# A gated recurrence with a multiplicative feed-forward: single PSUM banks for the first up product, two short leading chunks, a new division of copies among engines and a new written order

## The chip, the cores and the metric

The kernel runs on one core of one Trainium2 chip. A core has TensorE (PE: matrix products, its weight loads shown as PEld), VectorE (DVE), ScalarE (ACT), GpSimd (POOL), and SyncE (SP), which here issues almost all DMA transfers. The metric is the device time of one execution in microseconds; the median of five executions stands for the kernel.

## The reference

There are 4 sequences of 5,824 tokens with 256 channels, 23,296 tokens in all, in float32. First comes a recurrence over time, channel by channel, whose coefficients are gates:

```python
a_base = 1.0 / (1.0 + np.exp(-a_param))
log_a = c * sig_r * np.log(np.clip(a_base, 1e-06, 1.0 - 1e-06))[None, None, :]   # c = 8, sig_r = sigmoid(r_gate)
a_t = np.exp(log_a)
norm = np.sqrt(np.maximum(1.0 - a_t * a_t, 1e-06))
x_gated = norm * sig_i * x                                                       # sig_i = sigmoid(i_gate)
h = a_t[:, t] * h + x_gated[:, t]                                                # for every t, from h = 0
```

Its output, all h, goes through a feed-forward with a product in place of an activation; the widths are 256, 1024, 1024, 256:

```python
a = x @ w1
b = x @ w2
h = a * b @ w3
return (h @ w_out).astype(np.float32)
```

## The kernel before

**Tiles.** The tokens are cut into chunks: one of 256 and 45 of 512 (list `sizes`, L50). For the recurrence channels must lie on partitions and time along the row, so a chunk is held as two channel blocks of 128 partitions; `cb` counts them. The inputs come with tokens on partitions, so the two gate terms are turned by 128 x 128 blocks: on TensorE against an identity (`turn_pe`, L162) for the chunks in the sets `TURN_R` and `TURN_U`, and by a transposing DMA (`turn_dma`, L174) for the others.

**One chunk, step by step.** Each step has a letter in the order list. `r`, `i`, `x` load the inputs (L118). `R` and `I` are tanh of half the gates on ScalarE (a sigmoid is half of one plus such a tanh). `p` adds one (GpSimd), `t` multiplies by x in two halves (GpSimd; VectorE does both steps in one for the chunks in `DV_TIMES`). `V` and `U` turn the results. `d` is the decay, an exponential on ScalarE, whose per-channel rate stands in `la4`; `s` squares it (GpSimd, or VectorE where `DV_SQUARE` says so); `q` is the root of one minus the square (ScalarE); `g` multiplies by the turned gate (VectorE); `h` is the scan over time (VectorE, L214), which starts from the last column of the chunk before; `y` casts to bfloat16 (GpSimd, or VectorE for `DV_CAST`). The exponential and tanh on one side and the root on the other need different function tables of ScalarE, which are loaded at each turn from one to the other.

**Feed-forward of a chunk.** The 1,024 hidden columns are taken in four pairs of 128-column blocks; `mp` is the pair. `a` makes the pair of the first product with w1 (four matmuls of 128 x 128 weights and up to 512 tokens), `b` that with w2 (L240). `c` copies a finished `a` from PSUM to SBUF as bfloat16, on ScalarE or, for the pairs in `DV_COPY`, on VectorE (L256). `m` multiplies the copy by `b` straight from PSUM (VectorE, L262). `D` multiplies 128 tokens of the product by the folded matrix (8 matmuls of 256 columns, L269), `e` copies two such results out of PSUM (ScalarE, or VectorE for `DV_EVAC`), and `o` stores them. w3 and w_out aren't applied one after the other: at the start their product is computed once (`Ft`, `Fc`, `Fm`, `Fe`), and `D` uses that.

**PSUM.** [...] A ring of three double-bank tiles, `pab`, is shared by `a`, `b` and the warming matmuls (`warm`, L235); a ring of two single banks, `po`, serves the turns on TensorE, the folding and `D`. A tile is given out again after its reader is done, in the order of allocation.

**Order.** Nothing is scheduled automatically. `ORDER` is a written list of some 2,000 steps (2,450 in the changed kernel, where `a` and `c` come in halves); each engine takes its own instructions from it in exactly that order and waits at an instruction until its inputs, and its buffer, are ready. So the list settles what stands behind a late step on the same engine. Its beginning is `A0. r1 r0 i0 Lw3.0 x0 i1 A1. E R1 R0 x1 V0 V1 ...`, where `Lw`/`Cw` load and cast pieces of weights and `A0`, `A1`, `A2` compute the rates from `a_param`, which a small transfer on ScalarE's queue brings in single words, one per channel.

Of the kernel before, what the change touches and what calls it, by code (L numbers as in the profile page):

```python
# [10 lines left out]
F32 = mybir.dt.float32  # L11
# [11 lines left out]
def kernel(  # L23
# [26 lines left out]
    sizes = [256] + [CT] * 45  # L50
# [10 lines left out]
    psum = ctx.enter_context(tc.tile_pool(name="psum", bufs=3, space=bass.MemoryType.PSUM))  # L61
# [6 lines left out]
    la4 = consts.tile([P, NCB], F32, tag="la4")  # L68
    zz, zd, zt = (consts.tile([P, NCB], F32, name=tag, tag=tag) for tag in ("zz", "zd", "zt"))
# [9 lines left out]
    TURN_R = {0, 1, 2, 3, 4, 5, 7, 8, 13}  # L79
    TURN_U = {0, 1, 2, 3, 5, 8, 9}  # L80
    DV_TIMES = {0, 1, 2, 8}
    DV_PLUS = set()
    DV_HALF = set()
    DV_SQUARE = {(0, 0), (0, 1), (1, 0), (1, 1), (5, 0), (6, 0), (7, 1), (9, 1), (11, 0), (12, 0), (14, 0), (15, 1),
        (20, 1), (24, 1), (27, 0), (29, 0), (36, 0), (37, 0), (38, 0), (41, 0)}
    DV_CAST = {0, 20, 28, 37, 39, 40, 42, 45}
    DV_COPY = {(0, 3), (1, 1), (1, 3), (2, 1), (3, 2), (7, 2), (8, 0), (8, 1), (10, 0), (11, 1), (13, 0), (14, 0),
        (14, 2), (15, 3), (18, 1), (18, 3), (19, 3), (20, 3), (21, 3), (22, 3), (23, 1), (25, 0), (25, 2), (28, 1), (33,
        1), (33, 2), (36, 3), (40, 2), (41, 2), (41, 3), (44, 0), (45, 0)}
    DV_EVAC = {(0, 0), (1, 1), (2, 0), (2, 1), (3, 0), (4, 0), (4, 1), (5, 0), (6, 1), (7, 1), (8, 1), (9, 1), (10,  # L90
        0), (17, 0), (18, 1), (19, 0), (19, 1), (22, 0), (23, 1), (27, 0), (27, 1), (28, 1), (30, 0), (31, 0), (33, 1),
        (34, 1), (35, 0), (35, 1), (41, 1), (42, 0), (42, 1)}
    FOLD_ACT = {('c', 7), ('e', 0), ('e', 1), ('e', 4), ('e', 6), ('e', 7)}
    W_ACT = {('w2', 0), ('w3', 1), ('w3', 2), ('w3', 3)}
    W_DVE = {('w3', 0)}
    STAGE = {'w1': ['a', 'a'], 'w2': ['nrm', 'nrm'], 'wo': ['a', 'nrm'], 'w3': ['a', 'nrm', 'a', 'nrm', 'a', 'nrm',
        'a', 'nrm']}
    WARM = [30, 30, 24]
    src = {"r": rf, "i": jf, "x": xf}

    def flat(t):
        return t.rearrange("p cb j q -> p (cb j q)").rearrange("p (j d) -> p j d", d=D)

# [22 lines left out]
    def tanh_r(c):  # L126
# [4 lines left out]
        else:  # L131
            nc.scalar.activation(out=t.rearrange("p cb j q -> p j cb q"), in_=cut(T["r", c]),  # L132
# [9 lines left out]
    def plus(c):  # L142
        t = T["thi", c]
        (nc.vector if c in DV_PLUS else nc.gpsimd).tensor_scalar(t, t, 1.0, 1.0, op0=ALU.add, op1=ALU.mult)  # L144
# [384 lines left out]
```

## Time and profile before

| what | value |
|---|---|
| median of 5 executions | 522.42 us (520.72 to 524.76) |
| the profiled execution | 523.5 us, span of the core 521.7 us |
| TensorE busy | 502.2 us (96% of the span) |
| VectorE busy | 479.8 us (92%) |
| ScalarE busy | 429.6 us (82%) |
| GpSimd busy | 299.3 us (57%) |
| DMA traffic | 123.28 MB, mean 236 GB/s; 83.8% of the 16 DMA engines' time on SP's queue |

The span is what the profiler saw on the core, from the first instruction to the last; the execution's own time is a little longer. A group in the profile reads: line, engine, operation, output<-inputs, sizes and count, then busy time and mean duration of one in ns, then the engine's idle time before these and what ended it. In a list of waits each row says who waited for whom: us in total, times, longest. Busy time of TensorE includes the ends of matmuls that overlap with the next one.

### The profile page before, as it was taken

The numbers are of one execution on the slowest core, as the hardware profiler recorded it, in microseconds if no ns is written. First come the engines' busy times: TensorE is split into PE (matmuls) and PEld (weight loads), VectorE is DVE, ScalarE is ACT, GpSimd is POOL, SyncE is SP. The second block draws the span as 40 slices with busy tenths as digits, with TensorE's granted clock in tenths as the row PEclk, the third lists the DMA queues.
The fourth block names the chain that finished last, engine by engine and source line by source line (L and its number), as shares of the span: only waits on it lengthen the run. The fifth ranks groups of instructions, "written<-read, shape, count | busy, mean of one in ns | idle before, by whom it ended". The sixth has DMA issues, their size and how long they took to land.

```text
span 521.7 us, 8827 instructions
## 1 busy us (share of the span) xinstructions
PE 502.2 (96%) x3260; PEld 309.8 (59%) x3260; DVE 479.8 (92%) x456; ACT 429.6 (82%) x493; POOL 299.3 (57%) x251
## 2 busy tenths in 40 slices
PE   4899999999999999999999999999999999999997
PEld 4667655656565566566665556556556565656556
DVE  4899999999999999899999899999998999999973
ACT  6899997998898998999987997988977796766432
POOL 0668755786829674876566765757257756634000
PEclk9999999999999999999999999999999999999999
DMA  8999979899999886999979969999966978342113
GB/s 297 405 410 291 333 252 274 224 294 253 332 294 265 201 235 201 278 247 302 246 227 302 240 216 217 292 238 247 245 178 199 274 210 203 101 123 81 62 52 111
DMA packets 174604, 123.28 MB, mean 236 GB/s; under 512 B 84448, under 2 KB 170208, under 8 KB 174560
## 3 DMA queue, kind: packets, MB, share of 16 engines
q1 hardware_dynamic: 174288, 122.71, 83.8%
q8 instruction: 25, 0.41, 0.3%
q14 instruction: 19, 0.16, 0.1%
q10 hardware_dynamic: 272, 0.00, 0.0%
HBM read 78.91 MB, written 23.86 MB: 197 GB/s over the span
## 4 chain that ended last, share of the span: by engine, by line
PE 72%; DVE 15%; issue 6%; ACT 4%; DMA 2%; POOL 0%; SPq 0%; DVEq 0%; ACTq 0%; POOLq 0%
PE pb L246 23%; PE po L277 23%; PE pa L246 22%; DVE g_t L266 6%; DVE h_t L225 4%; DVE sa L252 1%; PE pw L342 1%; DVE nrm L210 1%; DMA i_t<-in_i_gate_dram 1%; ACT sa L254 1%; PE warm L238 1%; DMA la<-in_a_param_dram 1%; ACT a_t L188 1%; PE ptr L167 1%; DVE nrm L195 1%
## 5 line engine op out<-in xcount | busy, mean ns | idle before, releaser
L246 PEld LDWEIGHTS <-w_sb 128*128 128x128 bf16 x1472 | 143.0, 98 | 152.7 <-issue 12.7
L266 DVE TENSOR_TENSOR g_t<-sa,pb 128x1024 bf16<-128x1024 bf16 (+1 forms) x184 | 216.0, 1199 | 16.9 <-PE pb L246 10.7
L254 ACT CAST sa<-pa 128x1024 bf16<-128x1024 f32 (+1 forms) x152 | 149.7, 1004 | 55.0 <-PE pa L246 50.7
L246 PE MATMUL pb<-y_t,w_sb 128*128 128x512 bf16 (+1 forms) x736 | 180.2, 377 | 5.0 <-DVE g_t L266 2.5
L246 PE MATMUL pa<-y_t,w_sb 128*128 128x512 bf16 (+1 forms) x736 | 180.7, 377 | 3.5 <-DVE g_t L266 1.6
L277 PE MATMUL po<-wp_sb,g_t 128*128 128x256 bf16 x1456 | 179.4, 273 | 0.0
L277 PEld LDWEIGHTS <-g_t 128*128 128x128 bf16 x1456 | 142.4, 98 | 42.4 <-issue 0.2
L225 DVE TENSOR_TENSOR_SCAN h_t<-a_t,h_t,nrm 128x512 f32<-128x512 f32 (+3 forms) x90 | 117.7, 1334 | 1.2
L160 POOL TENSOR_TENSOR u_t<-th_i,x_t 128x512 bf16<-128x512 f32 x84 | 113.2, 1364 | 2.5 <-DMA ut<-u_t 1.3
L233 POOL CAST y_t<-h_t 128x1024 bf16<-128x1024 f32 x38 | 44.4, 1169 | 119.2 <-DVE h_t L225 102.6
L195 POOL TENSOR_TENSOR nrm<-a_t 128x512 f32<-128x512 f32 x72 | 85.5, 1200 | 20.7 <-ACT a_t L188 20.6
L144 POOL TENSOR_SCALAR th_i<-th_i 128x1024 f32<-128x1024 f32 x42 | 49.2, 1174 | 30.8 <-ACT th_i L139 30.7
L188 ACT ACTIVATE a_t<-rt,la 128x512 f32<-128x512 bf16 x74 | 59.1, 819 | 2.6 <-DMA rt<-th_r 1.5
L139 ACT ACTIVATE th_i<-i_t 128x1024 f32<-128x1024 f32 (+1 forms) x46 | 48.3, 1052 | 7.6 <-DMA i_t<-in_i_gate_dram 3.9
L210 DVE SCALAR_TENSOR_TENSOR nrm<-nrm,ut 128x1024 f32<-128x1024 f32 x39 | 52.7, 1354 | 0.0
L254 ACT COPY ot<-po 128x512 f32<-128x512 f32 (+1 forms) x60 | 34.7, 578 | 17.0 <-PE po L277 16.2
L199 ACT ACTIVATE nrm<-nrm 128x1024 f32<-128x1024 f32 (+1 forms) x46 | 46.9, 1048 | 0.3
L252 DVE CAST sa<-pa 128x1024 bf16<-128x1024 f32 (+1 forms) x32 | 38.3, 1198 | 5.6 <-PE pa L246 5.4
L132 ACT ACTIVATE th_r<-r_t 128x1024 bf16<-128x1024 f32 x37 | 39.3, 1061 | 0.1
L199 ACT ACT_TABLE_LOAD x20 | 25.7, 1283 | 1.7 <-DVE nrm L195 1.4
L252 DVE COPY ot<-po 128x512 f32<-128x512 f32 (+1 forms) x33 | 21.9, 665 | 4.0 <-PE po L277 4.0
L195 DVE TENSOR_TENSOR nrm<-a_t 128x512 f32<-128x512 f32 (+1 forms) x20 | 18.5, 931 | 0.9 <-ACT a_t L188 0.9
(51 smaller groups left out, 157.0 us busy)
## 6 DMA issues: line engine op xcount, KB each, us to landing
r_t<-in_r_gate_dram SPq DMA_DIRECT2D x45, 512.0 KB, 5.6
i_t<-in_i_gate_dram SPq DMA_DIRECT2D x45, 512.0 KB, 5.4
x_t<-in_x_dram SPq DMA_DIRECT2D x45, 512.0 KB, 5.5
out_dram<-ot SPq DMA_DIRECT2D x89, 256.0 KB, 3.6
wf<-in_moe_w_dram SPq DMA_DIRECT2D x12, 512.0 KB, 9.0
wf<-in_moe_w_out_dram SPq DMA_DIRECT2D x2, 512.0 KB, 11.5
ut<-u_t SPq DMA_TRANSPOSE x39, 4.9
rt<-th_r SPq DMA_TRANSPOSE x37, 4.5
```

The source lines that it names most:

```text
L144: (nc.vector if c in DV_PLUS else nc.gpsimd).tensor_scalar(t, t, 1.0, 1.0, op0=ALU.add, op1=ALU.mult)
L160: (nc.vector if (c, half) in DV_HALF else nc.gpsimd).tensor_mul(out=u, in0=t, in1=xt)
L188: nc.scalar.activation(out=a, in_=pr, func=AF.Exp, scale=la4[:, cb:cb + 1], bias=la4[:, cb:cb + 1])
L195: eng.tensor_mul(out=T["n", c][:, cb, :w], in0=T["a", c][:, cb, :w], in1=T["a", c][:, cb, :w])
L199: nc.scalar.activation(out=T["n", c][:, :, :w], in_=T["n", c][:, :, :w], func=AF.Sqrt, scale=-1.0, bias=1.0)
L210: nc.vector.scalar_tensor_tensor(out=T["n", c][:, :, :w], in0=T["n", c][:, :, :w], scalar=1e-3, in1=T["pu", c][:, :, :w], op0=ALU.max, op1 ...
L225: nc.vector.tensor_tensor_scan(T["h", c][:, cb, lo:hi], T["a", c][:, cb, lo:hi], T["n", c][:, cb, lo:hi], init, ALU.mult, ALU.add)
L246: nc.tensor.matmul(out=pp[:, q, :w], lhsT=w_sb[:, cb, m * P:(m + 1) * P], rhs=T["y", c][:, cb, :w], start=(cb == 0), stop=(cb == NCB - 1))
L252: nc.vector.tensor_copy(out=dst, in_=src_ps)
L254: nc.scalar.copy(out=dst, in_=src_ps)
L266: nc.vector.tensor_mul(out=T["g", c][:, 2 * mp:2 * mp + 2, :w], in0=T["sa", c, mp][:, :, :w], in1=T["pb", c, mp][:, :, :w])
L277: nc.tensor.matmul(out=po, lhsT=T["g", c][:, k, j * P:(j + 1) * P], rhs=wp_sb[:, k, :], start=(k == 0), stop=(k == KD - 1), skip_group_che ...
```

## The change

There are five parts.

1. **PSUM.** The ring of three double banks becomes two rings: `psum_a`, two single banks for halves of the first product, and `psum_b`, two double banks for the second product and the warming. The step `a` is issued in halves (`a12.0.1` is chunk 12, pair 0, half 1), and so is its copy `c`. The eight banks remain in use.
2. **Chunks.** The sizes are 256, 256, 44 times 512 and 256. So the first two chunks and the last are short, and there are 47. Several helpers take the chunk's length where they had the full one (`dense`, `plus`, `times`, `turn_dma`).
3. **Division of work.** ScalarE gets a list of squares, `AC_SQUARE` (17 of them). The sets for VectorE shrink: output copies from 33 to 5, squares from 20 to 4, casts of y from 8 to none, and first-product copies from 32 pairs to 44 halves, all in chunks 0 to 10. TensorE turns r for 7 chunks (9 before) and u for 6 (7 before). The casts of the weights move between engines.
4. **Rates.** `a_param` comes as two rows of 128 words, is turned on TensorE (`rates_turn`) and copied to `la4`. There are four sets of warming identity products (26, 16, 24, 36 matmuls; before 30, 30, 24).
5. **Order.** The whole list is new.

`CASTING` and `AC_CAST` are empty sets, so the branches that ask for them don't run.

```diff
-    sizes = [256] + [CT] * 45
+    sizes = [256, 256] + [CT] * 44 + [256]
...
-    psum = ctx.enter_context(tc.tile_pool(name="psum", bufs=3, space=bass.MemoryType.PSUM))
+    psum_a = ctx.enter_context(tc.tile_pool(name="psum_a", bufs=2, space=bass.MemoryType.PSUM))
+    psum_b = ctx.enter_context(tc.tile_pool(name="psum_b", bufs=2, space=bass.MemoryType.PSUM))
     psum_o = ctx.enter_context(tc.tile_pool(name="psum_o", bufs=2, space=bass.MemoryType.PSUM))
...
-    TURN_R = {0, 1, 2, 3, 4, 5, 7, 8, 13}
-    TURN_U = {0, 1, 2, 3, 5, 8, 9}
-    DV_TIMES = {0, 1, 2, 8}
+    TURN_R = {0, 1, 2, 3, 4, 7, 9}
+    TURN_U = {0, 1, 2, 3, 4, 7}
+    DV_TIMES = {0, 1}
...
+    DV_HALF = {(2, 0), (15, 0)}
+    DV_SQUARE = {(1, 0), (1, 1), (3, 1), (14, 1)}
+    AC_SQUARE = {(0, 0), (0, 1), (2, 0), (2, 1), (4, 0), (4, 1), (7, 0), (7, 1), (8, 0), (9, 1), (10, 1), (11, 1),
+        (12, 0), (13, 1), (14, 0), (15, 1), (16, 0)}
+    DV_CAST = set()
...
+    DV_EVAC = {(1, 0), (6, 0), (9, 0), (9, 1)}
...
-    W_ACT = {('w2', 0), ('w3', 1), ('w3', 2), ('w3', 3)}
-    W_DVE = {('w3', 0)}
+    W_ACT = {('w2', 1), ('w3', 4), ('w3', 7)}
+    W_DVE = {('w1', 0), ('w1', 1), ('w2', 0)}
...
-    WARM = [30, 30, 24]
+    WARM = [26, 16, 24, 36]
...
+        if (c, cb) in AC_SQUARE:
+            nc.scalar.activation(out=n, in_=a, func=AF.Square)
+        else:
+            (nc.vector if (c, cb) in DV_SQUARE else nc.gpsimd).tensor_mul(out=n, in0=a, in1=a)
...
+    def up(c, m, dst, w_sb):
+        w = sizes[c]
+        for cb in range(NCB):
+            nc.tensor.matmul(out=dst[:, :w], lhsT=w_sb[:, cb, m * P:(m + 1) * P],
+                             rhs=T["y", c][:, cb, :w], start=(cb == 0), stop=(cb == NCB - 1))
+
+    def up_a(c, mp, q):
+        T["pa", c, mp, q] = pp = psum_a.tile([P, CT], F32, name="pa", tag="pa")
+        up(c, 2 * mp + q, pp, w1_sb)
+
+    def up_b(c, mp):
+        T["pb", c, mp] = pp = psum_b.tile([P, 2, CT], F32, name="pb", tag="pb")
         for q in range(2):
...
+            up(c, 2 * mp + q, pp[:, q, :], w2_sb)
...
+    def copy(c, mp, q):
+        w = sizes[c]
+        if q == 0:
+            T["sa", c, mp] = ffn.tile([P, 2, CT], BF16, name="sa", tag="sa")
+        copy_to((c, mp, q) in DV_COPY, T["sa", c, mp][:, q, :w], T["pa", c, mp, q][:, :w])
...
+    def rates_turn():
+        pt = psum_b.tile([P, 2, CT], F32, name="pr_la", tag="pb")
+        nc.tensor.matmul(out=pt[:, 0, :NCB], lhsT=la_rows, rhs=ident_f[:NCB, :NCB], is_transpose=True,
+                         start=True, stop=True)
+        T["la"] = pt[:, 0, :NCB]
...
     ORDER = """
-        A0. r1 r0 i0 Lw3.0 x0 i1 A1. E R1 R0 x1 V0 V1 Lw1.1 Cw1.1 I0 A2. d0.0 d0.1 d1.0 d1.1 r2 Lw1.0 Lw2.0 Lw2.1 W1
-        I1 s0.0 Cw3.0 s0.1 t0.1 s1.0 s1.1 W0 U0 i2 Cw1.0 q0 t1.1 g0 h0.0 q1 R2 U1 Lw3.1 h0.1 y0 W2 a0.2 g1 h1.0 c0.2
...
+        r0 i1 r1 i0 E x0 x1 A3. A0. R0 A1. A2. W0 I1 V0 t1.1 I0 R1 d0.0 s0.0 d0.1 t0.1 V1 W1 U0 Lw1.0 r2 r3 d1.0 d1.1
+        s1.0 Cw1.0 Lw2.0 s0.1 Lw1.1 i2 W2 W3 Lw2.1 x2 s1.1 q0 g0 h0.0 h0.1 U1 y0 q1 g1 a0.0.0 h1.0 h1.1 R2 R3 a0.0.1
...
-    nc.scalar.dma_start(out=la4, in_=a_param.rearrange("(cb p) -> p cb", p=P))
+    nc.scalar.dma_start(out=la_rows, in_=a_param.rearrange("(cb p) -> cb p", p=P))
```

## The prediction

> **What bounds the kernel now.** I read the page's shares of busy time first, then busy time by stretch, the waits of TensorE, and the groups with their durations. The page, parts 1 and 2:
>
> ```profile
> PE 502.2 (96%) x3260; PEld 309.8 (59%) x3260; DVE 479.8 (92%) x456; ACT 429.6 (82%) x493; POOL 299.3 (57%) x251
> ...
> PE   4899999999999999999999999999999999999997
> ...
> DVE  4899999999999999899999899999998999999973
> ACT  6899997998898998999987997988977796766432
> ```
>
> TensorE is never idle for long, VectorE hardly, ScalarE is full early and loosens. A busy TensorE is not TensorE at its pace, so I take its work from starts. In the trace's list of instructions one matmul follows the next after 216 ns at 512 columns, 109 at 256, 56 at 128. Summed: up products 1,440 x 0.216 + 32 x 0.109 = 314.5; down products 1,456 x 0.109 = 158.7; weight folding 64 x (0.056 + 0.109) = 10.6; transposes 120 x 0.056 = 6.7; warming 84 x 0.083 = 7.0. Together 497.5 us. The span is 521.7 = 20.9 (TensorE's start and waits) + 497.5 + 3.3 (drain of the last matmul, copy, store). Start and waits stand at 11.9 by 28 us, 14.8 by 140, 15.4 by 300, 20.9 by 440, and grow no further. So the prize is in these 20.9; after the start they hold 9.0.
>
> Busy time by stretch (PE, weight loads, DVE, ACT, POOL, clock, DMA share, GB/s):
>
> ```profile
> 20.00:60.00 40.00, 38.76 (x314) 25.86 (x312) 38.11 (x44) 39.88 (x51) 27.90 (x26) 1.00 1.06 347
> 60.00:140.00 80.00, 78.46 (x506) 47.61 (x505) 78.23 (x77) 71.75 (x81) 55.30 (x46) 1.00 0.98 276
> 140.00:300.00 160.00, 159.75 (x987) 96.22 (x986) 152.41 (x137) 146.64 (x166) 106.49 (x89) 1.00 0.95 255
> 300.00:440.00 140.00, 135.78 (x831) 80.99 (x829) 131.77 (x113) 114.92 (x131) 84.98 (x67) 1.00 0.87 229
> ```
>
> From 20 to 60 us ScalarE is full: there it sets the pace. From 60 to 140 VectorE has 1.8 of 80 us free and ScalarE 8. Who makes TensorE wait:
>
> ```profile
> PE pb L246 <- DVE g_t L266: 2.5, 5, 1.2
> PE pa L246 <- DVE g_t L266: 1.6, 3, 0.6
> PE pa L246 <- DVE y_t L233: 1.5, 1, 1.5
> ...
> PE pb L246 <- DVE sa L252: 1.3, 1, 1.3
> PE pb L246 <- ACT sa L254: 0.9, 2, 0.5
> ```
>
> VectorE ends these waits for a PSUM buffer in 5.4 us, ScalarE in 0.9. The durations:
>
> ```profile
> L266 DVE TENSOR_TENSOR g_t<-sa,pb 128x1024 bf16<-128x1024 bf16 x180 | 213.3, 1211 | 16.9 <-PE pb L246 10.7 <-ACT sa L254 4.5 <-PE po L277 0.5
> L254 ACT CAST sa<-pa 128x1024 bf16<-128x1024 f32 x149 | 148.0, 1012 | 53.3 <-PE pa L246 49.0 <-issue 2.7 <-DVE g_t L266 1.1
> L254 ACT COPY ot<-po 128x512 f32<-128x512 f32 x58 | 33.9, 585 | 14.4 <-PE po L277 13.6 <-ACT ot L254 0.5
> L252 DVE CAST sa<-pa 128x1024 bf16<-128x1024 f32 x31 | 37.6, 1214 | 5.6 <-PE pa L246 5.4
> L199 ACT ACT_TABLE_LOAD x20 | 25.7, 1283 | 1.7 <-DVE nrm L195 1.4
> ```
>
> Neighbours overlap, so I price by start to start, median of those back to back: ScalarE copy 904 ns (1,024 columns), 476 (512), tanh 959, root 963, decay 717, table load 1,294; VectorE product 1,131, scan 1,195, copy 1,134 and 601. At these prices ScalarE has 416 us of work, VectorE 449, GpSimd 266.
>
> **What the Trainium skill says.** "TensorE: Matmul & The Clock Gate", Back-to-back issue gap: N/2.4 + 2.5 ns for one matmul after another when warm, 215.8 at 512; the trace's 216 agrees (its 131 ns for a pipelined stream doesn't). "ScalarE: Activation LUTs", What ACT_TABLE_LOAD costs: an ACTIVATE is 186 ns + 0.833 per column, each pointer operand 93 more, 93 overlapped. That gives 705 for a decay, 717 here; for a Square of 512 columns, which the trace lacks, 520 (estimate). Its drain of 1,380 ns after a table load isn't seen: 1,294 from load to next. "PSUM — Partial Sum Buffer", PSUM bank collisions raise a hardware error: TensorE and a reader must not share a bank. Before, the copy takes a pair of banks at once; single banks let TensorE refill one half while the other is read. No run so far shows that.
>
> **The change, part by part.**
>
> *TensorE.* Transposes 120 to 88: -1.8. Warming 84 to 102: +1.5. Three 256-token chunks for one: 64 x (2 x 0.109 - 0.216) / 2 = +0.1. Down products and folding unchanged. Sum 497.2.
>
> *ScalarE.* First-product copies: 149 x 0.904 + 3 x 0.476 = 136.1 become 319 x 0.476 + 13 x 0.265 = 155.3: +19.2. Output copies 58 to 86: +13.1. Squares 0 to 17: +8.4. Table loads 40 to 35: -6.5. Others about +1. Sum 416 to 451: it takes 35 us of load.
>
> *VectorE.* First-product copies 35.8 to 33 x 0.601 + 11 x 0.335 = 23.5: -12.3. Output copies 33 to 5: -16.6. Squares 20 to 4: -9.7. Casts of y 8 to 0: -4.6. Others about 0. Sum 449 to 406.
>
> *GpSimd* gets all casts of y (38 to 47), loses some squares: 266 to 279, far under 497. A cast takes 1.00 instead of 0.61 on VectorE; scans run several chunks ahead of their up products after the start, which hides the 0.4 us; without that lead it costs 0.4 a chunk, 3 us for eight. *SP* issues 81 transposes for 76 and, with one more chunk, 3 more loads. Along both lists the bytes asked for stand equally at equal TensorE work (38.5 MB at 126 us, 37.5 at 127), so I add nothing; uncovered, a late transfer shows at 4.5 to 5.6 us to land.
>
> *The start.* Chunk 0's root, gating and scans come before chunk 1's, both are short, and the decay rates arrive as two rows turned on TensorE, not as 256 single words (4.8 us to land). Tanh of r no longer stands behind them: before, ScalarE first computes at 5.72 us. I place it at 4 to 5.7 after. From there to the first up product: tanh and decays 5.5, table load and root 1.9, gating and scans 2.8, cast 0.6, so 15 to 16.6 against 17.86. But little stays. Adding ScalarE's work along the list up to where TensorE's sum is 26 gives 33.2, a lead of 6.8; before, 34.1 at 27.5, a lead of 6.6. TensorE's delay there is about ScalarE's start plus this lead: before 5.7 + 6.6 = 12.3, the trace 11.9. After 4.7 + 6.8 = 11.5. Gain 0.4; bounds 0 and 2.
>
> *The middle.* In the new list ScalarE's lead falls to 3.5 at 126, is about 0 at 185 and negative after: it may idle 3 us up to 126 and still not hold TensorE. VectorE's lead is 2 at most where I read it (67) and -26 at 251. The waits that VectorE ended (5.4) and those that follow a late product have a lighter engine behind them, and a second product now has its own two pairs of banks: TensorE returns to one after a median of 4.3 us of other work, before after 2.6 in the shared ring. Of 9.0 I leave 1.5.
>
> *The new wait.* A single bank of the first product comes round after two, not three, allocations. Of 374 reuses 129 have 1.30 us of TensorE work or less between. Its copy takes 0.48; the other 0.8 covers signals and whatever ScalarE is in the middle of: at most a tanh (0.96) or a table load (1.29). Behind the waiting matmul stand all later up and down products, and VectorE waits for those. Bounds: nothing, or 0.14 to 0.48 at each, 18 to 62 us. I take 2.0, 16 ns each, since in the whole trace ScalarE ended only 0.9 us of TensorE's waits at 151 reuses.
>
> Sum: 497.2 + 11.5 + 1.5 + 2.0 + 3.3 (tail: same last copies and stores) = 515.5 against 521.7. The profiled execution took 523.5, 1.8 over its span, and the median of the five runs 522.42 is 0.7 over the span: 515.5 + 0.7 gives 516.2; I say 516.5.
>
> **Rivals.** *Late ScalarE (slower).* Single banks put each half-copy on TensorE's path in the stretch where both are full (from 17 to 185 us of TensorE's work the list holds 98% as much for ScalarE). With 0.1 us at each of the 129 tight reuses: 497.2 + 11.5 + 1.5 + 12.9 + 3.3 = 526.4, median 527. It decides against the change from (20.9 + 0.3 - 13.0) / 129 = 64 ns. For: 40 us of ScalarE full in the trace before. Against: from 40 to 60 us TensorE lost 0.03 us beside a full ScalarE. *Late transfers (same).* DMA share is 0.95 to 1.06 from 20 to 300 us, and a new order can meet late loads and turns elsewhere; the waits only move: 497.2 + 11.5 + 9.0 + 3.3 = 521.0, median 521.7. Against: ScalarE waited only 5.4 us for DMAs in all. *Clean pass (faster still).* No wait after the start: 497.2 + 11.0 + 0.5 + 3.3 = 512.0, median 512.7. *The reserve is not used*: a lighter VectorE alone brings nothing where TensorE was at its pace (140 to 300 us, 0.6 lost); that is in the sum already.
>
> **How the numbers follow.** Chances: forecast 0.40, clean pass 0.13, waits that only move 0.22, late ScalarE 0.25. Half a per cent (2.6 us) is what a measurement can tell from no change: 519.8 to 525.0. The forecast and the clean pass lie below, the moved waits between, late ScalarE mostly above. Faster 0.53, same 0.23, slower 0.24. The range 511.5 to 527 reaches from the clean pass to 0.1 us at each tight reuse and leaves out wider losses; for the faster cases alone it is 511.5 to 519.8.
>
> **What would show it.** Right: start and waits of TensorE near 15 us; product waits (g_t before pb) below 1 us; ScalarE near 465 us busy, VectorE near 435; half-copies of 585 ns. Wrong: rows of pa waiting for ScalarE's copies above 8 us in sum between 30 and 200 us, or ScalarE waiting for transposes. A first up product later than 17 us would say that I have the start wrong.

## The result and the profile after

The changed kernel takes 523.18 us, median of 43 executions (520.71 to 526.24). The kernel before, run beside it and in all later comparisons, takes 521.19 us, median of 80. The ratio is 1.0033, 95% interval 1.0023 to 1.0042: slower by a third of a per cent, where 516.5 us was forecast. That is inside the half per cent I called "no change", and on the wrong side of it.

The profiled execution of the changed kernel has a span of 520.7 us. The page, parts 1 and 2:

```profile
PE 503.2 (97%) x3279; PEld 312.7 (60%) x3279; DVE 435.1 (84%) x424; ACT 466.8 (90%) x718; POOL 315.4 (61%) x267
...
PE   7889999998999999999899999998999999999997
...
DVE  5999999999998888789888598985789787759762
```

The work has moved as the diff says: VectorE from 479.8 to 435.1 us busy, ScalarE from 429.6 to 466.8. In tenths, TensorE's line is as it was, while VectorE's has fallen from 9 to mostly 7 or 8 after 150 us. Busy time by stretch of the changed kernel, the three later stretches (columns as before):

```profile
60.00:140.00 80.00, 78.01 (x488) 46.75 (x487) 78.17 (x81) 77.03 (x111) 50.07 (x42) 1.00 1.08 277
140.00:300.00 160.00, 158.06 (x969) 94.70 (x968) 136.92 (x112) 154.87 (x241) 116.73 (x93) 1.00 1.00 264
300.00:440.00 140.00, 138.01 (x851) 83.06 (x850) 114.83 (x96) 127.27 (x198) 91.69 (x74) 1.00 0.87 226
```

From 60 to 140 us VectorE is as full as before (78.2 of 80 us): its relief comes later. From 140 to 300 us it has 23 us free, where before it had 8, and yet TensorE was busy for 1.7 us less than before; from 300 to 440 for 2.2 us more. Two groups of the changed kernel, its products and its half-copies on ScalarE:

```profile
L289 DVE TENSOR_TENSOR g_t<-sa,pb 128x1024 bf16<-128x1024 bf16 x176 | 210.2, 1212 | 62.4 <-PE pb L261 29.0 <-ACT sa L277 25.5 <-ACT a_t L200 2.1
L277 ACT CAST sa<-pa 128x512 bf16<-128x512 f32 x319 | 179.2, 596 | 33.8 <-PE pa L261 28.5 <-DVE g_t L289 4.0
```

The first row tells where the 44 us of VectorE went. In front of its products VectorE was idle for 16.9 us before and is idle for 62.4 now: it arrives early and waits for TensorE's second product or ScalarE's copy. By this row it became idle time. The half-copies (mean 596 ns of one) wait for TensorE too. Who makes TensorE wait, the rows of the rings:

```profile
PE pa L261 <- DVE sa L275: 3.5, 5, 1.6
...
PE pb L261 <- DVE g_t L289: 2.6, 2, 1.9
PE pa L261 <- ACT sa L277: 2.2, 3, 1.5
```

Counted as in the prediction (time of a matmul's start less TensorE's work up to it), start and waits stand at 11.1 us by 45, 14.0 by 123, 14.2 by 240, 16.4 by 251, 18.4 by 370, 19.1 by 428 and 20.1 at the end. So the waits after the start are 9.0 us in the profiled execution, to the tenth what they were in the profiled one of before (which took 2.3 us more than the median, see below). And they are few. Looking for TensorE's gaps above 0.4 us after 45 us, I find six: 0.5 at 116, 1.7 at 120, 2.1 at 247, 1.7 at 360, 0.6 at 424, 0.8 at 484, together 7.3 of the 9.0. Four of them (4.4 us) stand in front of a first product, at its single banks: those at 116 and 120 behind a half-copy of VectorE, those at 360 and 424 behind one of ScalarE. The other two (2.9 us) wait for a bank of the second product, behind VectorE's multiply.

Each has a story of its own on another engine's queue. The largest one, VectorE's instructions one after another (start, us, what):

```profile
240.71 1.22 DVE L225 SCALAR_TENSOR_TENSOR nrm<-nrm,ut 128x1024 f32<-128x1024 f32 x1
241.84 3.26 DVE L240 TENSOR_TENSOR_SCAN h_t<-a_t,h_t,nrm 128x512 f32<-128x512 f32 x2
245.03 1.19 DVE L240 TENSOR_TENSOR_SCAN h_t<-a_t,nrm 128x128 f32<-128x128 f32 x1
246.14 1.72 DVE L240 TENSOR_TENSOR_SCAN h_t<-a_t,h_t,nrm 128x384 f32<-128x384 f32 x1
247.78 1.19 DVE L240 TENSOR_TENSOR_SCAN h_t<-a_t,nrm 128x128 f32<-128x128 f32 x1
248.90 2.32 DVE L289 TENSOR_TENSOR g_t<-sa,pb 128x1024 bf16<-128x1024 bf16 x2
```

A gating and five scans stand in one block (rows with x2 hold two instructions), 8.2 us from 240.71 to 248.90, and the product that frees TensorE's bank is behind them. One chunk there contains the border between two sequences, so its two scans are cut into four. But the cut alone doesn't make the block. GpSimd's instructions in that time, and VectorE's at an earlier border, at 138 us:

```profile
243.25 1.04 POOL L251 CAST y_t<-h_t 128x1024 bf16<-128x1024 f32 x1 [3.75 <-DVE h_t L240]
244.26 1.68 POOL L152 TENSOR_SCALAR th_i<-th_i 128x1024 f32<-128x1024 f32 x1
245.91 2.78 POOL L210 TENSOR_TENSOR nrm<-a_t 128x512 f32<-128x512 f32 x2
```

```profile
138.15 0.62 DVE L240 TENSOR_TENSOR_SCAN h_t<-a_t,h_t,nrm 128x192 f32<-128x192 f32 x1
...
139.91 0.80 DVE L240 TENSOR_TENSOR_SCAN h_t<-a_t,nrm 128x320 f32<-128x320 f32 x1
140.62 1.20 DVE L225 SCALAR_TENSOR_TENSOR nrm<-nrm,ut 128x1024 f32<-128x1024 f32 x1
```

At 138 us the four cut scans take 2.5 us together, with GpSimd idle; in the block, with GpSimd at work beside each of them, they take 5.7 (243.2 to 248.9). The wait at 120 us, VectorE's queue:

```profile
118.39 2.06 DVE L225 SCALAR_TENSOR_TENSOR nrm<-nrm,ut 128x1024 f32<-128x1024 f32 x1
120.38 1.52 DVE L171 TENSOR_TENSOR u_t<-th_i,x_t 128x512 bf16<-128x512 f32 x1
121.82 0.68 DVE L275 CAST sa<-pa 128x512 bf16<-128x512 f32 x1
```

A gating that takes 1.2 us elsewhere takes 2.06, then comes the half-multiply that the set `DV_HALF` gives VectorE for chunk 15 (1.52, against 0.68 for the one of chunk 2); GpSimd works beside both. Only then comes the half-copy for which TensorE's single bank waits. The wait at 360 us begins on SyncE's queue (its issues of transfers in order of time):

```profile
351.74 0.38 SPq L319 DMA_DIRECT2D out_dram<-ot  x1
352.17 1.10 SPq L129 DMA_DIRECT2D r_t<-in_r_gate_dram  x2
```

and ends on ScalarE's, where the brackets hold an idle time and who ended it:

```profile
360.62 1.06 ACT L140 ACTIVATE th_r<-r_t 128x1024 bf16<-128x1024 f32 x1 [1.76 <-DMA r_t<-in_r_gate_dram]
361.58 1.05 ACT L277 CAST sa<-pa 128x512 bf16<-128x512 f32 x2
```

After a load of x, issued by 348.5, SyncE stood for 3.3 us in front of a store, whose output copy ScalarE finished at 351.7; two loads of r behind it went out only at 352.17; one took 7.9 us to land; ScalarE waited 1.76 us for it; and the half-copies behind the tanh came late for TensorE. The waits at 424 (an output copy waits for a buffer of its ring of three) and 484 us (two scans that take 3.5 us, ahead of a product) are of the same kinds.

### The profile page after: what moved, and what is told of

Same layout as the page of the kernel before. It is cut to its first block, busy times and chain, and to the rows that moved or that the text cites. A ratio compares the mean times of both kernels' runs of the same rounds, so it can differ in the third digit from the quotient of the medians.

```text
span 520.7 us, 9046 instructions
## 1 busy us (share of the span) xinstructions
PE 503.2 (97%) x3279; PEld 312.7 (60%) x3279; DVE 435.1 (84%) x424; ACT 466.8 (90%) x718; POOL 315.4 (61%) x267
## 4 chain that ended last, share of the span: by engine, by line
PE 70%; DVE 8%; ACT 6%; issue 4%; DMA 4%; SPq 1%; POOL 1%; DVEq 0%; ACTq 0%; POOLq 0%
PE po L300 24%; PE pa L261 23%; PE pb L261 23%; DVE h_t L240 3%; DMA r_t<-in_r_gate_dram 3%; DVE g_t L289 3%; DMA out_dram<-ot 1%; ACT sa L277 1%; DVE sa L275 1%; DVE nrm L225 1%; ACT nrm L214 1%; PE pw L371 1%; ACT a_t L200 1%; ACT th_r L140 1%; ACT th_i L147 1%
## 5 line engine op out<-in xcount | busy, mean ns | idle before, releaser
L277 ACT CAST sa<-pa 128x512 bf16<-128x512 f32 (+1 forms) x332 | 183.8, 587 | 36.0 <-PE pa L261 30.3
L251 POOL CAST y_t<-h_t 128x1024 bf16<-128x1024 f32 (+1 forms) x47 | 52.3, 1113 | 120.2 <-DVE h_t L240 107.0
L240 DVE TENSOR_TENSOR_SCAN h_t<-a_t,h_t,nrm 128x512 f32<-128x512 f32 (+4 forms) x92 | 121.1, 1340 | 1.3
L171 POOL TENSOR_TENSOR u_t<-th_i,x_t 128x512 bf16<-128x512 f32 (+1 forms) x88 | 114.8, 1323 | 1.9 <-POOL nrm L210 0.3
L210 POOL TENSOR_TENSOR nrm<-a_t 128x512 f32<-128x512 f32 (+1 forms) x73 | 86.6, 1199 | 18.7 <-ACT a_t L200 18.7
L152 POOL TENSOR_SCALAR th_i<-th_i 128x1024 f32<-128x1024 f32 (+1 forms) x45 | 57.5, 1277 | 41.9 <-ACT th_i L147 39.6
L200 ACT ACTIVATE a_t<-rt,la 128x512 f32<-128x512 bf16 (+1 forms) x80 | 64.3, 825 | 0.1
L225 DVE SCALAR_TENSOR_TENSOR nrm<-nrm,ut 128x1024 f32<-128x1024 f32 (+1 forms) x41 | 54.5, 1328 | 0.7 <-DMA ut<-u_t 0.6
L140 ACT ACTIVATE th_r<-r_t 128x1024 bf16<-128x1024 f32 (+1 forms) x40 | 42.6, 1065 | 1.8 <-DMA r_t<-in_r_gate_dram 1.8
L275 DVE CAST sa<-pa 128x512 bf16<-128x512 f32 (+1 forms) x44 | 25.9, 615 | 1.3 <-PE pa L261 0.9
```

What stands on the lines that cost most here:

```text
L171: (nc.vector if (c, half) in DV_HALF else nc.gpsimd).tensor_mul(out=u, in0=t, in1=xt)
L200: nc.scalar.activation(out=a, in_=pr, func=AF.Exp, scale=la4[:, cb:cb + 1], bias=la4[:, cb:cb + 1])
L210: (nc.vector if (c, cb) in DV_SQUARE else nc.gpsimd).tensor_mul(out=n, in0=a, in1=a)
L225: nc.vector.scalar_tensor_tensor(out=T["n", c][:, :, :w], in0=T["n", c][:, :, :w], scalar=1e-3, in1=T["pu", c][:, :, :w], op0=ALU.max, op1 ...
L240: nc.vector.tensor_tensor_scan(T["h", c][:, cb, lo:hi], T["a", c][:, cb, lo:hi], T["n", c][:, cb, lo:hi], init, ALU.mult, ALU.add)
L277: nc.scalar.copy(out=dst, in_=src_ps)
```

## The experiments

All ratios are to the kernel before; the changed kernel's own is 1.0033.

**1. More work for VectorE, in the loop from copy to product.** In each chunk the product of pair 0 is written twice.

```diff
-        nc.vector.tensor_mul(out=T["g", c][:, 2 * mp:2 * mp + 2, :w], in0=T["sa", c, mp][:, :, :w],
...
+        for _ in range(2 if mp == 0 else 1):
+            nc.vector.tensor_mul(out=T["g", c][:, 2 * mp:2 * mp + 2, :w], in0=T["sa", c, mp][:, :, :w],
...
```

> The changed kernel, with the product of pair 0 of every chunk written twice by VectorE (same values): 47 products of 1.13 us more, so VectorE's work is about 459 us, more than the 449 before the change, and ScalarE's is as in the changed kernel. The changed kernel stands at 1.0033 of the kernel before. Local lateness (waits come from single late moments, VectorE's sum is free): 1.001 to 1.007, TensorE's waits after the start grow by less than 2 us. If VectorE's sum were what the change had bought: the 5 us or more that were forecast as its worth are lost, 1.013 or more.

Measured: 569.02 us, ratio 1.0907 (1.0866 to 1.0947). Far above local lateness, and far above the 5 us that the other expectation named as its least: of 53 us added, some 46 came through. The busy times on the page of this run, and the first row of TensorE's waits:

```profile
PE 512.0 (90%) x3224; PEld 311.5 (55%) x3279; DVE 493.2 (87%) x471; ACT 470.8 (83%) x718; POOL 315.1 (56%) x267
```

```profile
PE pb L261 <- DVE g_t L290: 27.0, 29, 3.0
```

VectorE is idle for 73 us in this run and still makes TensorE wait, 29 times for a bank of the second product. The loss is spread: 1 to 4 us in most stretches of 20.

**2. The same for ScalarE.** One half-copy of each chunk is made twice (22 us).

```diff
-        copy_to((c, mp, q) in DV_COPY, T["sa", c, mp][:, q, :w], T["pa", c, mp, q][:, :w])
+        for _ in range(2 if (mp, q) == (0, 1) else 1):
+            copy_to((c, mp, q) in DV_COPY, T["sa", c, mp][:, q, :w], T["pa", c, mp, q][:, :w])
```

> The changed kernel, with one half-copy of every chunk (pair 0, half 1) done twice: 47 x 0.476 = 22 us more, nearly all on ScalarE (451 to 472), VectorE as it was. In the changed kernel's trace ScalarE has idled about 1 us by 78 us and 4.6 by 140. Late ScalarE (its sum and the single banks hold TensorE): 5 us or more above the changed kernel, ratio 1.013 or more, and TensorE's waits grow all through to 250 us. Local lateness: only where ScalarE has no reserve, in the first 80 us, 2 to 3 us, ratio 1.007 to 1.010. Late transfers alone: 1.003.

Measured: 539.79 us, ratio 1.0355 (1.0336 to 1.0373); 17 of 22 us come through. The number is where late ScalarE put it, and from 140 to 250 us ScalarE is full in this run (108.8 of 110 us busy). But its fullness isn't the whole reason: some 6 of the 17 us are lost after 240, and from 300 to 440 ScalarE is busy for 131.4 of 140. TensorE's waits for ScalarE's half-copies rise from 2.2 to 6.0 us in the whole run.

**3. Fewer transfers.** No loads of i and x after chunk 4: the later chunks use the tiles of chunk 4, so their gated inputs are other ones (43.5 of 78.9 MB of reads are left out).

```diff
     def load(c, nm):
+        if nm in "ix" and c > 4:
+            T[nm, c] = T[nm, 4]
+            return
```

> The changed kernel without the loads of x and the input gate after chunk 4: these chunks use chunk 4's tiles, so 42 MB of 98 and some 84 transfers are left out and the values are others; all work of the engines stays. Late transfers alone: TensorE's waits after the start fall from 9.0 to below 2, ratio 0.988 or less. Local lateness: the two waits that a load and a store ended (2.2 us) and part of the others go, the waits behind VectorE stay, 2 to 4 us less, ratio 0.995 to 0.999. Late ScalarE: less than 1 us, 1.002 or more.

Measured: 521.07 us, ratio 0.9997 (0.9988 to 1.0007), 2.1 us less than the changed kernel: between two of the expectations and near local lateness. The waits at 360 and 424 us are gone; those at 120 (2.0), 247 (2.1) and 482 us (0.8) stay. Transfers are a quarter of the 9.0, not their cause as a whole.

**4. No border.** The scans aren't cut at the borders between sequences, so the state runs on from one sequence into the next (another computation).

```diff
-        cuts = [0] + [b * S - starts[c] for b in range(1, B) if 0 < b * S - starts[c] < w] + [w]
+        cuts = [0, w]
```

> The changed kernel, with the recurrence run through the three borders between sequences: the scan is not cut and not started from zero there, so six scans are left out and the values after a border are others. In the changed kernel's trace four scans in a row at the second border took 5.75 us and TensorE lost 2.1 us behind them. Local lateness: 1.5 to 2.5 us less, ratio 0.9985 to 1.0005, and no wait of TensorE near 247 us. Late transfers alone, late ScalarE: unchanged, 1.003.

Measured: 521.89 us, ratio 1.0003 (0.9991 to 1.0014), as local lateness said. The wait at 247 us is gone; those at 121, 359 and 482 stay, and the small one at 424 isn't there. Six scans fewer, 1.3 us won.

**5. The doubled product in the kernel before.** The edit of run 1, in the old list with its shared ring of three.

> The kernel before (old rings, old list) with the product of pair 0 of every chunk written twice by VectorE: 46 more products, +52 us of VectorE at 1.13 us each, the same edit that cost the changed kernel 45 of 53 us. VectorE's starts sum to 449 + 52 = 501 us, against 497.5 of TensorE. Theory A (it is the place that counts: a product more in the way from a copy to the return of a second-product bank passes through in any list that was written this tightly): +40 us or more, ratio 1.075 to 1.11. Theory B (the new rings of two are what makes the changed kernel so stiff, the old shared ring of three takes up most): VectorE's sum alone is the bound, 501 + 20 of start and tail, +10 to +25 us, ratio 1.02 to 1.05.

Measured: 571.49 us, ratio 1.0957 (1.0922 to 1.0992). 50 of 52 us come through; the new rings are no stiffer than the old. (VectorE is 94% busy in this run, so here its total has a part in it too, which run 1 excludes for the changed kernel.)

**6. Casts of y on VectorE.**

```diff
-    DV_CAST = set()
+    DV_CAST = set(range(47))
```

> The changed kernel with all 47 casts of y given back to VectorE: +28 us for VectorE (0.61 each), -47 us for GpSimd, nothing else moved. VectorE's sum becomes 434, under the 449 of the kernel before. Theory A (place counts): the casts stand behind scans and in front of products, 0.6 us each; a good part passes through, +5 to +20 us, ratio 1.01 to 1.04. Theory B (VectorE has a reserve of 43 us against before, and uses 28 of it here): within 2 us of the changed kernel, ratio 1.000 to 1.007. Theory C (GpSimd [...] is what stretches VectorE's scans, so fewer GpSimd reads pay): faster than the changed kernel, ratio below 1.000, scans shorter on the mean.

Measured: 556.99 us, ratio 1.0691 (1.0651 to 1.0731). Worse than all three. The move was mis-sized: a cast takes 1.02 us on the mean on VectorE, not 0.61, and VectorE's busy time grew by 49 us, not 28. That cost 34 us, though VectorE, 87% busy, still had time to spare. The scans didn't get shorter (mean 1.48 us). The cast stands behind two scans and in front of everything that follows, and TensorE waited 11.6 us for y itself.

**7. Output copies on VectorE.**

```diff
-    DV_EVAC = {(1, 0), (6, 0), (9, 0), (9, 1)}
+    DV_EVAC = {(1, 0), (6, 0), (9, 0), (9, 1)} | {(c, 1) for c in range(10, 46)}
```

> The changed kernel with 36 of its output copies (second half of chunks 10 to 45) given back to VectorE: VectorE +22 us to 428, ScalarE -17 us to 434, the division of this work about as before. Theory A (place counts): each such copy stands 0.6 us in front of a product; +3 to +12 us, ratio 1.009 to 1.027. Theory B (sums count, and both stay under TensorE's 497): no change against the changed kernel, ratio 1.001 to 1.006. Theory C (ScalarE's 35 us more are what keeps the expected gain away): 2 us or more faster than the changed kernel, ratio below 0.999.

Measured: 534.87 us, ratio 1.0242 (1.0200 to 1.0284): the place, and a lighter ScalarE bought nothing. The largest single loss, 3.8 us of TensorE at 201, on VectorE's queue:

```profile
201.63 3.18 DVE L240 TENSOR_TENSOR_SCAN h_t<-a_t,h_t,nrm 128x512 f32<-128x512 f32 x2
204.74 0.66 DVE L275 COPY ot<-po 128x512 f32<-128x512 f32 x1
```

A copy of 0.66 us cost 3.8: here it stands behind two scans, and the changed kernel, with this copy on ScalarE, shows no wait at this place.

**8. The few waits taken away, first try.** Borders: the decay of the border's column is set to zero, and one scan goes over the chunk. (The state before it is multiplied by zero, so the result is the same.) Further: six output buffers, stores 30 steps later, the half-multiply of chunk 15 on GpSimd, one scan of chunk 45 behind a product.

```diff
-    DV_HALF = {(2, 0), (15, 0)}
+    DV_HALF = {(2, 0)}
...
             (nc.vector if (c, cb) in DV_SQUARE else nc.gpsimd).tensor_mul(out=n, in0=a, in1=a)
+        for b in range(1, B):
+            if 0 < b * S - starts[c] < w:
+                nc.gpsimd.memset(T["a", c][:, cb, b * S - starts[c]:b * S - starts[c] + 1], 0.0)
...
-        cuts = [0] + [b * S - starts[c] for b in range(1, B) if 0 < b * S - starts[c] < w] + [w]
+        cuts = [0, w]
...
-        T["ot", c, j2] = ffn.tile([P, 2, D], F32, name="ot", tag="ot")
+        T["ot", c, j2] = ffn.tile([P, 2, D], F32, name="ot", tag="ot", bufs=6)
...
```

> The changed kernel with its few single waits taken away where they arise: at the three borders between sequences the decay of the border's column is set to zero and one scan goes over the whole chunk, not two (the result is the same, six scans fewer); six buffers for the output tiles, not three, and each store 30 steps later in the list, so that the queue of loads doesn't stand behind an output copy; the one half-multiply of chunk 15 on GpSimd, not VectorE; one scan of chunk 45 behind a product. Theory A (the waits after the start are four or five separate events, each with a local cause: 1.7 us at 120, 2.1 at 247, 1.7 at 360, 0.6 at 424, 0.8 at 484): 3.5 to 6 us faster than the changed kernel, ratio 0.990 to 0.996. Theory B (take a wait away and another comes, since some engine always ends late): ratio 0.999 to 1.004.

Measured: 523.12 us, ratio 1.0036 (1.0026 to 1.0046), what theory B gave. The waits at 247, 360, 424 and 484 us were gone, but others had come: 2.3 us at 98, and more at 80 to 140 and 280. The one at 98 I had written myself; GpSimd's queue of this run:

```profile
94.95 0.10 POOL L213 MEMSET a_t<- 128x1 f32 x1 [6.21 <-ACT nrm L208]
...
99.37 1.04 POOL L254 CAST y_t<-h_t 128x1024 bf16<-128x1024 f32 x1
```

A memset of 0.10 us has to wait until ScalarE has squared the column, 6.2 us; behind it stand an addition, a multiply by x and the cast of y, which in the changed kernel starts at 96.12 and here at 99.37, and TensorE waits for that. The later waits stood behind transposes that landed late; that the moved stores did it wasn't tried apart.

**9. VectorE lighter at the crowded places.** No gating from chunk 5 on; the scan takes the bare root (another computation).

```diff
     def gated(c):
         w = sizes[c]
+        if c > 4:
+            return
```

> The changed kernel without the gating step on VectorE from chunk 5 on (42 multiplies, -47 us for VectorE at 1.13 us each; the scan takes the bare root, so the computation is another one). It takes VectorE's work out where it piles up, between scans and in front of products. Theory A (TensorE's waits of the middle are VectorE late at a few places): the waits at 120 (1.7 us), 247 (2.1) and 484 us (0.8) go, those on loads and stores (2.2) stay; -3 to -5 us against the changed kernel, ratio 0.993 to 0.998. Theory B (the waits come from transfers and ScalarE, or new ones come for those that go): within 1.5 us of the changed kernel, ratio 1.000 to 1.007.

Measured: 516.98 us, ratio 0.9925 (0.9913 to 0.9938): 6.2 us less than the changed kernel, more than expected. The waits at 120, 424 and 484 us are gone, 1.0 is left at 247 and 0.4 at 357. So a lighter VectorE does pay, with about as much work as bought nothing in the change (47 us by price, 44 there), if the work goes from between the scans and the products. (GpSimd is busy for 20 us less in this run, too, and what that is worth wasn't tried apart.)

**10. GpSimd lighter.** It doesn't add one to tanh of i from chunk 5 on (another computation).

```diff
     def plus(c):
+        if c > 4:
+            return
```

> The changed kernel without the step on GpSimd that adds one to tanh of i from chunk 5 on (42 operations, -44 us for GpSimd; another computation). It leaves VectorE's work alone but takes away a good fifth of GpSimd's operations on SBUF, beside which VectorE's scans and gatings are stretched (scans 1.40 us on the mean against 1.26 undisturbed). Theory A (the stretching adds to VectorE's lateness at the few places): scans below 1.37 us, 1 to 3 us faster than the changed kernel, ratio 0.997 to 1.001. Theory B (stretching is spread and costs nothing): no change, ratio 1.002 to 1.005.

Measured: 520.98 us, ratio 0.9998 (0.9984 to 1.0011), 2.2 us less than the changed kernel, as theory A said; VectorE's scans take 1.35 us on the mean instead of 1.40, and the wait at 120 us is gone. Those at 246 (2.3), 361 and 484 us stay.

**11. The few waits taken away, second try.** As 8, but VectorE sets the border's column to zero, and the stores stay, save one that is put behind the two loads of r at 352 us.

```diff
...
-        cuts = [0] + [b * S - starts[c] for b in range(1, B) if 0 < b * S - starts[c] < w] + [w]
+        cuts = [0, w]
+        for b in range(1, B) if cb == 0 else ():
+            if 0 < b * S - starts[c] < w:
+                nc.vector.memset(T["a", c][:, :, b * S - starts[c]:b * S - starts[c] + 1], 0.0)
...
-        s37.0 p37 g33 h33.0 h33.1 a31.2.1 a31.1.1 d37.1 c31.1.1 b31.2 x36 m31.1 D29.2 c31.2.1 o29.0 r41 r39 a31.3.0
+        s37.0 p37 g33 h33.0 h33.1 a31.2.1 a31.1.1 d37.1 c31.1.1 b31.2 x36 m31.1 D29.2 c31.2.1 r41 r39 o29.0 a31.3.0
...
-        D41.3 a43.1.1 e41.0 a43.2.0 c43.1.1 o40.1 g45 c43.2.0 h44.1 h45.0 D42.0 b43.1 m43.1 e41.1 x46 a43.3.0 a43.3.1
+        D41.3 a43.1.1 e41.0 a43.2.0 c43.1.1 o40.1 g45 c43.2.0 h44.1 D42.0 b43.1 m43.1 h45.0 e41.1 x46 a43.3.0 a43.3.1
```

> As the run of few waits, but with the two things undone that brought new waits there: the border's column is set to zero by VectorE just ahead of the scan (GpSimd, which had to wait 6.2 us for a square on ScalarE, held up a cast of y by it, and TensorE waited 2.1 us for that), and the stores stay where they were, but for one that is set behind two loads of r at 352 us. Theory A (the waits are separate events): those at 247, 360, 424 and 484 us go, 5 us in sum, and at 120 a part; ratio 0.991 to 0.996. Theory B (others come for them): 0.998 to 1.004.

Measured: 516.73 us, ratio 0.9918 (0.9904 to 0.9933). It computes what the reference asks and is the fastest kernel of this study, 6.5 us under the changed one and 4.4 under the one before. The border at 243 us on VectorE's queue, and the two loads of r on SyncE's:

```profile
243.24 0.06 DVE L236 MEMSET a_t<- 128x2 f32 x1
243.42 4.03 DVE L243 TENSOR_TENSOR_SCAN h_t<-a_t,h_t,nrm 128x512 f32<-128x512 f32 x2
247.37 2.32 DVE L292 TENSOR_TENSOR g_t<-sa,pb 128x1024 bf16<-128x1024 bf16 x2
```

```profile
347.02 1.15 SPq L129 DMA_DIRECT2D r_t<-in_r_gate_dram  x2
350.22 0.90 SPq L322 DMA_DIRECT2D out_dram<-ot  x2
```

The product is free to start at 247.37, 1.5 us earlier, and the loads of r go out 5 us earlier. TensorE's waits for the rings in this run:

```profile
PE pa L264 <- DVE sa L278: 2.9, 6, 1.3
...
PE pa L264 <- ACT sa L280: 0.3, 1, 0.3
PE pb L264 <- DVE g_t L292: 0.2, 1, 0.2
```

Of these 0.5 us stand after 45 us. Counted as above, the waits after the start are 2.7 us, not 9.0. VectorE is 432.6 us busy and ScalarE 466.8, all but the same as in the changed kernel. The five edits weren't tried one by one; the border alone is run 4.

**12 and 13. VectorE's idle time filled.** In front of 17 products at which the changed kernel's trace shows VectorE idle, 38 multiplies that nobody reads (run 12); then 17 of them in 13 places (run 13).

```diff
...
+        for _ in range(FILL.get((c, mp), 0)):
+            nc.vector.tensor_mul(out=spare, in0=w1_sb[:, 0, :CT], in1=w1_sb[:, 1, :CT])
         if mp == 0:
```

> The changed kernel with 38 more multiplies of 512 columns on VectorE, written in front of those 17 products at which the trace of the changed kernel shows VectorE idle for 1.4 to 3.2 us; about 0.6 us each, 23 us in all, each place filled to at most 0.4 us under its idle time. They read a weight matrix and write a spare tile, so nothing waits for them but VectorE's own queue. Theory A (the place decides, not VectorE's sum): 0 to 5 us over the changed kernel, ratio 1.003 to 1.012. Theory B (VectorE's sum is what counts, 0.86 us of time for each us of work as with the doubled products, 1.2 as with the casts): +20 us or more, ratio 1.04 to 1.06.

> As the run that fills VectorE's idle time, with 17 spare multiplies in 13 places, not 38 in 17: those took 1.18 us each on the mean, not 0.6 (13 of them 0.69, the others up to 1.75 beside GpSimd), and overfilled the places. Now about 20 us are added, each place to at least 0.3 us under its idle time at 1.15 us each. Theory A (the place decides): 0 to 2 us over the changed kernel, ratio 1.002 to 1.008. Theory B (VectorE's sum counts at the rate of the doubled products): +17 us, ratio above 1.03.

Measured: 533.02 us, ratio 1.0227 (1.0206 to 1.0249), and 523.55 us, ratio 1.0045 (1.0031 to 1.0059). The groups of VectorE, of run 12 first:

```profile
L291 DVE TENSOR_TENSOR spare<-w_sb 128x512 f32<-128x512 bf16 x38 | 44.7, 1177 | 0.7
```

```profile
L294 DVE TENSOR_TENSOR g_t<-sa,pb 128x1024 bf16<-128x1024 bf16 x176 | 210.1, 1212 | 40.9 <-PE pb L264 17.5 <-ACT sa L280 16.9 <-PE po L305 1.9
L291 DVE TENSOR_TENSOR spare<-w_sb 128x512 f32<-128x512 bf16 x17 | 20.9, 1226 | 0.1
```

Run 12 was mis-sized: its multiplies took twice what I had planned, overfilled the places, and cost 10 us for 45. In run 13, 20.9 us of VectorE in the right places cost 0.4 us, no more than the intervals can tell from nothing, and the idle time in front of products fell from 62.4 to 40.9 by about that much. On the same engine 53 us of work took 46 us of time in run 1. It is the place.

**14. The kernel before without cuts at the borders.** The zeroed column of run 11 in the old list, nothing else.

> The kernel before with its scans uncut at the borders between sequences (the border's column of the decay set to zero by VectorE, the result is the same), nothing else: six scans fewer, VectorE's work 4 us less of 449. Theory A (the kernel before, too, lost time after the start in single pile-ups on VectorE, of which the border at 374 to 378 us with 2.0 us was one, so its waits had no relation to VectorE's sum): 1.3 to 2.5 us faster than before, ratio 0.995 to 0.9975. Theory B (VectorE's sum set the waits before): 4 us of 449 change nothing that can be seen, ratio 0.999 to 1.001.

Measured: 519.62 us, ratio 0.9968 (0.9956 to 0.9980), 1.7 us won, as theory A said. VectorE's queue in the kernel before:

```profile
369.25 4.29 DVE L225 TENSOR_TENSOR_SCAN h_t<-a_t,h_t,nrm 128x512 f32<-128x512 f32 x3
...
373.92 2.32 DVE L266 TENSOR_TENSOR g_t<-sa,pb 128x1024 bf16<-128x1024 bf16 x2
376.16 0.87 DVE L225 TENSOR_TENSOR_SCAN h_t<-a_t,h_t,nrm 128x320 f32<-128x320 f32 x1
376.96 1.32 DVE L225 TENSOR_TENSOR_SCAN h_t<-a_t,nrm 128x192 f32<-128x192 f32 x1
378.20 1.19 DVE L252 CAST sa<-pa 128x1024 bf16<-128x1024 f32 x1
```

TensorE lost 2.0 us there (at 374 and 378), waiting for products and for the copy at 378.20. The same block in run 14:

```profile
372.59 2.32 DVE L269 TENSOR_TENSOR g_t<-sa,pb 128x1024 bf16<-128x1024 bf16 x2
374.84 1.27 DVE L228 TENSOR_TENSOR_SCAN h_t<-a_t,h_t,nrm 128x512 f32<-128x512 f32 x1
376.03 1.19 DVE L255 CAST sa<-pa 128x1024 bf16<-128x1024 f32 x1
```

The copy comes 1.1 us after the scan's start, where before it came 2.0 after, and TensorE loses 1.1 us here, not 2.0. So this wait of the old list was a pile-up of the same kind, and about half of it went with 3 us of VectorE work (479.8 us busy to 476.6), not with 44. Of the 1.7 us won the two traces place these 0.9; where the rest was won they don't show.

The PSUM part alone wasn't tried. (As I read it, the new list, which hands out the halves in an order of its own, would lock up with the old ring of three; that wasn't run.) What the single banks are worth by themselves stays open.

## Why the prediction was wrong

**The work of each engine: right.** ScalarE was forecast near 465 us busy and has 466.8, VectorE near 435 and has 435.1; half-copies 477 ns from start to start (476 used), Squares 531 (520 was the estimate from the Trainium skill, "ScalarE: Activation LUTs", What ACT_TABLE_LOAD costs). TensorE's spacing is 216, 109 and 56 ns as before.

**The start: right.** Start and waits are 11.1 us by 45, forecast 11.5. The first up product comes at 14.3 us, earlier than the 15 to 16.6 worked out, and the first down product at 51.1 against 50.8 before: the gain is eaten, as the step said. It named ScalarE's lead; of TensorE's waits for first-product banks before 45 us, 1.6 us stand behind VectorE's half-copies and 0.3 behind ScalarE's. In eight more traces with the same beginning (runs 3, 4, 8 to 13) that first down product comes at 50.8 to 52.8.

**The new wait of the single banks: near in number, by luck.** Forecast 2.0 for ScalarE's copies, measured 2.2 in the row of pa waiting for ScalarE. But it isn't 16 ns at each of 129 reuses: 1.5 of it is the one late load at 360 us. And the step thought of ScalarE alone, though 44 half-copies are VectorE's: pa waited 3.5 us for these, 1.9 of it after 45 us. The rival of a late ScalarE, 0.1 us at each of 129 reuses, didn't come.

**"Of 9.0 I leave 1.5": this step failed.** With the new wait it made 3.5 us after the start; measured are 9.0. These 5.5 are the miss of 5.2 in the span (520.7 against 515.5; the start gives 0.4 back, the work is 0.1 more). With ScalarE's two gaps of 2.2 set apart, 6.8 us are left where 1.5 was forecast, and 5.1 of them are the four gaps behind VectorE. The step reasoned from leads and sums: the waits that VectorE ended "have a lighter engine behind them". From 60 to 140 us, where TensorE lost 3.0 us, that engine wasn't lighter at all. Where it was, from 140 to 300 us, TensorE had lost only 0.6 before, as the rival of a reserve that isn't used said. And VectorE takes its instructions in the written order: what TensorE waits for is how much stands in front of one product or copy at one moment. Copies, casts and squares taken off VectorE in the old list didn't thin the places where gatings and scans stood in a row ahead of a product; a new list made new such places. Three observations show it: 20.9 us put into VectorE's idle places cost 0.4 us (run 13); 53 us put in the way cost 46 (run 1); and with five local edits that leave the engines' sums nearly as they are, the waits after the start fall to 2.7 us (run 11), somewhat below the 3.5 I had forecast, and the time to 516.73. What I had forecast from a lighter VectorE was to be had, but by order.

**The rival "late transfers, the waits only move": right in number for the profiled execution, wrong in its cause.** It gave a span of 521.0, measured 520.7. Of the 7.3 us in six gaps, 2.2 begin with a transfer (360 and 424 us), 5.1 on VectorE; run 3 took away 2.1 us and no more.

**The base: 1.8 us.** I set the profiled span 0.7 under the median of five. An execution lasts 1.8 us longer than its span, and the profiled one of before was slower than most: 523.5 against a median of 521.19 over 80. So its waits were probably some 2 us more than usual; the 0.7 us that TensorE lost at 90 and the 1.4 at 436 are absent from the trace of run 14, whose list is the same. So less was to be won than the profile showed. The changed kernel's profiled execution was 0.7 faster than its median. Together: 515.5 forecast span + 5.2 + 2.5 to the median = 523.2. This also says why the change is slower: worked out from the medians (less 1.8, TensorE's work and the tail of 3.3), start and waits are 18.6 us before and 20.8 in the changed kernel, an estimate. They grew by 2.2 us while the work fell by 0.2; that the two profiled executions show 9.0 each tells nothing of this.

The sign that I had named, product waits (g_t before pb) below 1 us, was the right one to look at: it is 2.6. What I hadn't looked at is that VectorE's block of scans, with the border in it, was in the diff to be read: `g23 h22.1 h23.0` stand in the new list, and chunk 23 holds a border.

## What to carry to other kernels

Where each engine takes its instructions in a written order and buffers come in rings of two or three, an engine's sum of work tells only that it isn't the bound; a wait is worth what stands in front of the late instruction in its own queue at that moment. List the bottleneck engine's gaps one by one, look at the block in front of each releaser and at what works beside it, and move or shorten that block; then look for what the edit itself now waits for, as with the 0.10 us memset that held up GpSimd for 6.2. And set the base by the median of many executions, not by the profiled one.

## What the runs showed of the hardware

**VectorE and GpSimd stretch each other, to double and more.** The spare multiply of run 12, two inputs in SBUF, takes 0.69 us when GpSimd is still (11 cases, 683 to 693 ns), and mostly 1.4 to 1.75 us with a GpSimd operation beside it. In the changed kernel scans of 512 columns take 1.27 us undisturbed (51 cases) and 1.61 on the mean beside GpSimd (31); the product, which takes one input from PSUM, is never stretched (mean 1,212 ns). GpSimd's addition of one takes 1.04 us at 98 us, beside a product, and 2.01 at 119, beside a gating. This agrees with the Trainium skill, "SBUF — State Buffer", Who interferes with whom: a VectorE instruction with two SBUF inputs contends with a GpSimd instruction that reads SBUF. I hadn't priced it; run 10 puts a part of it, GpSimd's additions, at about 2 us here.

**A border is dear beside GpSimd, and hardly elsewhere.** Start to start, the four cut scans of a border chunk take 2.5 us at 138 and at 381 us, where GpSimd is still, and 5.7 at 243. Uncut (run 11), the chunk's two scans take 2.4 us at 138 and 4.0 at 243. So at 243 us cutting costs 1.7 us and GpSimd the rest. The memset that does without the cut takes 0.06.

**Two half-copies cost 954 ns against 904 for a whole one.** That is 50 ns of ScalarE for each pair.
